# Moving large loads and the start of the score bursts into the first matmul of each group: attention and MLP on one core

## The chip, the cores and the metric

The kernel runs on one core of a Trainium2 chip. The metric is device microseconds of one execution. A run is told with a state: "fast", "slow" (over 1.5% above the fastest run of the same kernel), or "unknown" for a single look. Each experiment was timed beside the kernel before on the same chip. A ratio below is the mean time of one kernel's fast runs over the mean of the other's fast runs of the same rounds, so it is not quite the ratio of the medians that stand beside it. In the views, PE is TensorE's matmuls, PEld its weight loads, DVE is VectorE, ACT ScalarE, POOL GpSimd and SP SyncE; L340 is line 340 of that run's kernel.

## The reference

Two steps, cut to what matters. First attention for 8 batches of 8 heads, 576 positions, 64 wide, in two parts that are added: a local one (each position sees neighbours closer than 4) and one on means of 4 positions. Then an MLP on the 4,608 tokens.

```python
q_d, k_d, v_d = (t.reshape(B, H, S // 4, 4, D).mean(axis=3) for t in (q, k, v))
out_up = np.repeat(sm_attn(q_d, k_d, v_d), 4, axis=2)
mask = np.abs(pos[:, None] - pos[None, :]) < 4
out_local = softmax(where(mask, scale * q @ k.T, -1e9)) @ v
x = (out_up + out_local).transpose(0, 2, 1, 3).reshape(B * S, H * D)   # 4608 x 512
h = x @ w_in                                                            # 512 -> 2048
out = (h * sigmoid(1.702 * h)) @ w_out                                  # 2048 -> 512
```

## The kernel before

The MLP runs in nine groups of 512 tokens. A group has `mm1` (64 matmuls of 512 columns, then SiLU on ACT) and `mm2` (64 more). While group g runs, the attention of batch g+1 is put between the matmuls of `mm2`, as bursts of many small matmuls: `scores` and `scores_d` for each half of the heads (called qd 0 and 1; 104 small matmuls each), `av` (44 for each of four head pairs), `transp` (28 each). Every matmul is two TensorE instructions, a weight load and a matmul (the trace has 5,148 of each).

```python
    def mm2(g, gT, steps):
        # ... cut
        for t, ffc in order:
            for f in steps.get(n, ()):
                f()                       # a burst of attention, ahead of matmul n
            n += 1
            # ... one 512-column matmul; every 16th: copy out and store

    POS = [0, 18, 25, 32, 43, 52]         # s0, s1, av(0,1), av(2,3), tr(0,1), tr(2,3)

    for g in range(n_groups):
        b = g + 1
        # ... g == 0 cut
        elif b < B:
            if b + 1 < B:
                for qd in range(NQ):
                    load_qk(b + 1, qd)    # POOL's queue; fp32 to bf16
            prep_qk(b, 0)                 # DVE transposes
            pool_qk(b, 0)                 # POOL: sums of four
            prep_v(b, nc.gpsimd)
            if b + 1 < B:
                load_v(b + 1)             # SP's queue, 256-byte pieces
            prep_qk(b, 1)
            pool_qk(b, 1)
            prep_v4(b, nc.gpsimd)
            if b + 1 < B:
                load_v4(b + 1)            # SP's queue, 1,024-byte pieces
        gT = mm1(g)
        # ... steps from POS, cut
        mm2(g, gT, steps)
```

Note where POOL meets `load_qk(b + 1)`: in program order at the start of a group, but POOL has by then done the `prep_v4` of the group before, so it issues these loads as soon as that is finished, in the middle of the group before (in the group from 164.12 us, from 180.78 us on).

The softmax here doesn't subtract the row's maximum and nothing guards it: scores larger than these inputs give would overflow.

## Time and profile before

| | before |
|---|---|
| median of fast runs (first three / beside the changed kernel) | 368.75 / 367.67 us |
| span of the profiled run | 367.2 us |
| PE busy | 86% |
| four groups with a long gap | 40.8, 39.4, 38.8, 38.3 us |
| the group with attention and no gap, from 241.16 us | 33.6 us |

The page in 40 slices: busy tenths of PE, and the clock that TensorE was granted.

```profile
PE   0224899959978999699969997999999999999996
...
PEclk9998699977998999699989999899999999999999
```

PE has dents at slices 11, 16, 20 and 24 (counted from 0), and the clock drops at or beside some of them. The table of PE's waits (what waited, for whom: us in total, times, longest) names them:

```profile
PE sl_194 L273 <- DVE vf L517: 11.6, 1, 11.6
PE av L340 <- issue: 9.3, 4, 3.3
...
PE av L326 <- issue: 6.0, 2, 3.2
PE xt L379 <- issue: 3.3, 2, 2.4
```

"issue" means that nothing the profile shows was waited for. The chain of waits around one gap (start us, us, what; L326 and L340 are the two halves of `av`):

```profile
184.48 1.62 PE ops L492 x7
186.09 0.28 PE av L326 x20
186.38 0.19 PE av L340 x24
...
186.94 3.32 issue
190.27 0.26 PE av L340 x2
```

The table by stretches (window, length; busy us and instructions of PE, weight loads, DVE, ACT, POOL; granted clock, DMA share, GB/s) for the time around that gap, then for three groups:

```profile
183.00:187.00 4.00, 3.94 (x199) 2.52 (x197) 1.27 (x4) 3.36 (x5) 0.00 (x0) 1.00 1.14 199
187.00:190.00 3.00, 0.00 (x0) 0.00 (x0) 1.01 (x1) 0.39 (x1) 0.00 (x0) 1.00 1.09 245
190.00:194.00 4.00, 3.73 (x57) 1.46 (x61) 1.34 (x2) 0.28 (x1) 0.00 (x0) 0.57 0.64 122
```

```profile
124.75:164.12 39.37, 36.25 (x625) 17.96 (x624) 15.14 (x25) 20.90 (x32) 17.34 (x19) 0.91 0.58 122
...
202.89:241.16 38.27, 35.50 (x625) 17.51 (x624) 15.04 (x25) 20.90 (x32) 17.33 (x19) 0.96 0.64 126
241.16:274.73 33.57, 33.57 (x625) 16.96 (x624) 14.94 (x25) 20.90 (x32) 15.23 (x15) 1.00 0.47 108
```

PE did nothing for 3 us while the DMA engines were full, and then ran at 0.57 of its clock for the next 4 us. The same work takes 33.57 us where there is no gap. The queues in 183 to 191 us (packets, MB, share of the time of 16 engines) show who filled the engines: q/k on the software queue, v4 on the hardware queue, and a single packet of the queue called "instruction":

```profile
q0 software_dynamic: 446, 0.93, 62.2%
q1 hardware_dynamic: 731, 0.81, 49.7%
q8 instruction: 1, 0.02, 0.7%
```

The prologue, in the chain: v is issued at 11.61 us and lands at 24.2; the MLP starts in earnest at 40.65.

```profile
10.48 1.08 DVE qT_146 L200
...
11.61 0.72 SPq L153
...
18.41 5.81 DMA vf<-in_v_dram
...
40.65 0.58 PE hps L465
```

### The profile page before, as it was taken

The numbers are of one execution on the slowest core, as the hardware profiler recorded it, in microseconds if no ns is written. First come the engines' busy times: TensorE is split into PE (matmuls) and PEld (weight loads), VectorE is DVE, ScalarE is ACT, GpSimd is POOL, SyncE is SP. The second block draws the span as 40 slices with busy tenths as digits, with TensorE's granted clock in tenths as the row PEclk, the third lists the DMA queues.
The fourth block names the chain that finished last, engine by engine and source line by source line (L and its number), as shares of the span: only waits on it lengthen the run. The fifth ranks groups of instructions, "written<-read, shape, count | busy, mean of one in ns | idle before, by whom it ended". The sixth has DMA issues, their size and how long they took to land.

```text
span 367.2 us, 11384 instructions
## 1 busy us (share of the span) xinstructions
PE 315.8 (86%) x5148; PEld 157.5 (43%) x5148; DVE 130.3 (35%) x219; ACT 180.8 (49%) x278; POOL 134.1 (37%) x157
## 2 busy tenths in 40 slices
PE   0224899959978999699969997999999999999996
PEld 0313344533444445344535454445544454444442
DVE  4727540276034802463136513460473163000000
ACT  1322373734760668146733675267636746623621
POOL 5871077007920396009900791069009700000000
PEclk9998699977998999699989999899999999999999
DMA  7499975998894149712991099317710011002002
GB/s 126 103 183 208 210 152 80 225 216 158 167 196 102 60 91 188 174 42 65 190 206 60 32 180 199 90 54 153 151 61 30 2 61 59 2 29 87 2 29 86
DMA packets 63265, 41.37 MB, mean 113 GB/s; under 512 B 44016, under 2 KB 54000, under 8 KB 63216
## 3 DMA queue, kind: packets, MB, share of 16 engines
q1 hardware_dynamic: 54912, 27.01, 32.6%
q0 software_dynamic: 8304, 13.63, 21.0%
q8 instruction: 40, 0.66, 0.8%
q14 instruction: 9, 0.07, 0.1%
HBM read 44.83 MB, written 9.44 MB: 148 GB/s over the span
## 4 chain that ended last, share of the span: by engine, by line
PE 82%; issue 6%; DVE 5%; ACT 2%; SPq 2%; DMA 2%; POOL 1%; DVEq 0%; POOLq 0%; ACTq 0%
PE ops L492 36%; PE hps L465 34%; PE av L340 2%; PE av L326 2%; DVE y L354 2%; SPq L153 2%; PE xt L368 2%; PE sd L289 2%; DMA vf<-in_v_dram 2%; PE xt L379 1%; PE vdp L246 0%; DVE xT_84 L406 0%; DVE vb_86 L224 0%; ACT osb L500 0%; DVE xT_85 L406 0%
## 5 line engine op out<-in xcount | busy, mean ns | idle before, releaser
L492 PE MATMUL ops<-w_out_bf,gT 128*128 128x512 bf16 x576 | 137.7, 393 | 0.0
L471 ACT ACTIVATE gT<-hps 128x512 bf16<-128x512 f32 x144 | 86.0, 597 | 44.7 <-PE hps L465 44.7
L465 PEld LDWEIGHTS <-w_in_bf 128*128 128x128 bf16 x576 | 57.0, 99 | 73.4 <-issue 8.5
L492 PEld LDWEIGHTS <-gT 128*128 128x128 bf16 x576 | 54.6, 100 | 65.4 <-issue 7.0
L465 PE MATMUL hps<-xT_84,w_in_bf 128*128 128x512 bf16 x144 | 55.7, 387 | 0.9 <-DVE xT_84 L412 0.9
L465 PE MATMUL hps<-xT_85,w_in_bf 128*128 128x512 bf16 x144 | 55.7, 387 | 0.5 <-DVE xT_85 L412 0.5
L465 PE MATMUL hps<-xT_82,w_in_bf 128*128 128x512 bf16 x144 | 56.1, 390 | 0.0
L465 PE MATMUL hps<-xT_83,w_in_bf 128*128 128x512 bf16 x144 | 56.0, 389 | 0.0
L500 ACT ACTIVATE osb<-ops 128x512 f32<-128x512 f32 x36 | 21.4, 597 | 67.6 <-PE ops L492 50.2
L390 ACT COPY od<-xt 128x576 f32<-128x576 f32 x32 | 19.1, 641 | 42.8 <-PE xt L379 42.8
L314 DVE TENSOR_TENSOR es_90<-es_90,mask 128x600 bf16<-128x600 bf16 x8 | 4.3, 536 | 89.8 <-ACT es_90 L300 89.8
L354 DVE TENSOR_TENSOR y<-av,rc 128x896 bf16<-128x896 f32 x32 | 34.9, 1092 | 1.1
L352 DVE RECIPROCAL rc<-av 128x14 f32<-128x14 f32 x32 | 7.7, 240 | 29.6 <-PE av L340 29.6
L368 PE MATMUL xt<-ident,y 60*64 60x57 bf16 (+1 forms) x640 | 10.5, 201 | 3.4 <-DVE y L354 3.2
L314 DVE TENSOR_TENSOR es_92<-es_92,mask 128x600 bf16<-128x600 bf16 x8 | 4.2, 531 | 25.1 <-ACT es_92 L300 25.1
L368 PEld LDWEIGHTS <-y 60*64 60x64 bf16 x640 | 8.2, 115 | 9.0 <-DVE y L354 5.3
L379 PE MATMUL xt<-ident,y 36*64 36x36 bf16 x256 | 8.1, 188 | 3.3 <-issue 3.3
L273 PE MATMUL sl_194<-qT_146,kT_144 32*64 32x60 bf16 x40 | 0.9, 242 | 11.6 <-DVE vf L517 11.6
L224 POOL CAST vb_87<-vf 128x2560 bf16<-128x2560 f32 x4 | 9.3, 2318 | 4.1 <-DMA vf<-in_v_dram 4.1
L424 ACT ACT_TABLE_LOAD x8 | 10.3, 1283 | 0.9 <-PEq L586 0.7
L436 ACT ACT_TABLE_LOAD x8 | 10.3, 1283 | 0.1
L406 DVE TENSOR_TENSOR xT_82<-xt,od 128x570 bf16<-128x570 f32 x8 | 6.0, 752 | 9.8 <-ACT od L390 9.8
(319 smaller groups left out, 361.1 us busy)
## 6 DMA issues: line engine op xcount, KB each, us to landing
vf<-in_v_dram SPq DMA_DIRECT2D x80, 128.0 KB, 3.7
out_dram<-osb SPq DMA_DIRECT2D x36, 256.0 KB, 2.1
v_96<-in_v_dram SPq DMA_DIRECT2D x36, 192.0 KB, 6.4
w_out_bf<-in_moe_w_out_dram POOLq DMA_DIRECT2D x4, 512.0 KB, 17.8
w_in_bf<-in_moe_w_in_dram POOLq DMA_DIRECT2D x2, 512.0 KB, 7.5
w_in_bf<-in_moe_w_in_dram POOLq DMA_DIRECT2D x1, 1024.0 KB, 13.2
kb_100<-in_k_dram POOLq DMA_DIRECT2D x1, 288.0 KB, 4.6
qb_102<-in_q_dram POOLq DMA_DIRECT2D x1, 288.0 KB, 5.3
```

What stands on the lines that cost most here:

```text
L224: eng.tensor_copy(out=vbs[b % 2][:, :, :, 0:D], in_=vf[b])
L314: nc.vector.tensor_tensor(out=ev, in0=ev, in1=mask, op=ALU.mult)
L354: nc.vector.tensor_tensor(out=y, in0=ov[:, :, :, 0:D], in1=rc.to_broadcast([128, 2, 7, D]), op=ALU.mult,)
L368: nc.tensor.matmul(x[64 * j : 64 * j + 64, par, 57 * i + c0 : 57 * i + c1], lhsT=y[64 * pos : 64 * pos + 60, par, i, :], rhs=ident[64 * po ...
L379: nc.tensor.matmul(x[64 * j : 64 * j + 64, xx, 288 + 36 * c2 : 324 + 36 * c2], lhsT=y[64 * pos : 64 * pos + 36, j, 5 + c2, :], rhs=ident[6 ...
L390: nc.scalar.copy(out=od.rearrange("p (x t f) -> p x t f", x=2, f=4), in_=x[:, :, 288:360, None].to_broadcast([128, 2, 72, 4]),)
L424: nc.scalar.preload_act_table_set("exp_and_others")
L436: nc.scalar.preload_act_table_set("silu_and_others")
L465: nc.tensor.matmul(hps, lhsT=w_in_bf[:, dmc, ffc * 128 : (ffc + 1) * 128], rhs=xT[dmc][:, tok0 : tok0 + TG], start=(dmc == 0), stop=(dmc = ...
L471: nc.scalar.activation(out=gT[:, ffc, :], in_=hps, func=AF.Silu, scale=GELU_SCALE)
L492: nc.tensor.matmul(ops[t], lhsT=gT[:, ffc, t * 128 : (t + 1) * 128], rhs=w_out_bf[:, ffc, :], start=(ffc == 0), stop=(ffc == n_ffc - 1),)
L500: nc.scalar.activation(out=osb, in_=ops[t], func=AF.Copy, scale=1.0 / GELU_SCALE)
```

## The change

The intent: the queue called "instruction" moved 40 packets of 16,384 B in the kernel before, which I read as TensorE's own instruction fetches. So let the bursts, which use up instructions fast (199 matmuls in 183 to 187 us, where large ones alone are some 18 in 4 us), run when few long transfers are in flight. Three things are done. The q/k loads of the next batch go behind `pool_qk(b, 0)`, and v4 is loaded at the start of its own group. The first score burst starts in `mm1` (slot 13 of 16), and the later positions move. In the prologue and group 0, constants that are needed late are made late, and the first v load no longer waits for the q transpose.

```diff
-        F = {}
+        # iotas reordered: those of the mask first (cut)
+        return dp, dr, di
+
+    def late_constants(dp, dr, di):
         nc.vector.tensor_single_scalar(out=ident, in_=di, scalar=0.0, op=ALU.is_equal)
         # ... rv, psel (cut)
@@ attention @@
-        return [s0, s1, avn(0, 1), avn(2, 3), tr(0, 1), tr(2, 3)]
+        return [lambda: s_pe(0), lambda: s_act(0), s1, avn(0, 1), avn(2, 3), tr(0, 1), tr(2, 3)]
-    def mm1(g):
+    def mm1(g, steps):
         for ffc in range(n_ffc):
+            for f in steps.get(ffc, ()):
+                f()
-    POS = [0, 18, 25, 32, 43, 52]
+    POS = [13, 16, 35, 40, 47, 54, 62]    # 16 is the first matmul of mm2
@@ prologue @@
-    constants()
-    prep_qk(0, 0)
+    late = constants()
+    prep_1("k", 0, 0)
+    load_v(0, gate=lambda t: nc.vector.memset(t, 0.0))
+    prep_1("q", 0, 0)
     pool_qk(0, 0)
-    load_v(0, gate=lambda t: nc.vector.memset(t, 0.0))
@@ groups @@
         elif b < B:
-            if b + 1 < B:
-                for qd in range(NQ):
-                    load_qk(b + 1, qd)
+            load_v4(b)
             prep_qk(b, 0)
             pool_qk(b, 0)
+            if b + 1 < B:
+                for qd in range(NQ):
+                    load_qk(b + 1, qd)
             prep_v(b, nc.gpsimd)
             # ... load_v, prep_qk(b, 1), pool_qk(b, 1) as before (cut)
             prep_v4(b, nc.gpsimd)
-            if b + 1 < B:
-                load_v4(b + 1)
```

More of the change, by code (lines that the diff above doesn't have):

```diff
@@ L79, in constants @@
         it = dict(allow_small_or_imprecise_dtypes=True)
+        halves = [slice(0, 64), slice(64, 128)]
         for par in range(2):
-            sl = slice(64 * par, 64 * par + 64)
-            nc.gpsimd.iota(dm[sl], pattern=[[-1, 60]], base=-4 * par,
+            nc.gpsimd.iota(dm[halves[par]], pattern=[[-1, 60]], base=-4 * par,
                            channel_multiplier=1, **it)
-            nc.gpsimd.iota(dp[sl], pattern=[[114, 5], [-192, 3], [-4, 64]],
+        for par in range(2):
+            nc.gpsimd.iota(dp[halves[par]], pattern=[[114, 5], [-192, 3], [-4, 64]],
                            base=KSTART[par], channel_multiplier=1, **it)
-            nc.gpsimd.iota(di[sl], pattern=[[-1, 64]], base=0,
+        nc.gpsimd.iota(dr, pattern=[[0, 1]], base=0, channel_multiplier=1, **it)
+        for par in range(2):
+            nc.gpsimd.iota(di[halves[par]], pattern=[[-1, 64]], base=0,
                            channel_multiplier=1, **it)
-        nc.gpsimd.iota(dr, pattern=[[0, 1]], base=0, channel_multiplier=1, **it)
         for t in kdT:
@@ L194, with prep_1 @@
     qT, kT, qdT = {}, {}, {}
-    def prep_qk(b, qd):
-        for name, store, dst in (("k", kf, kT), ("q", qf, qT)):
-            tt = work.tile([128, S, 2], BF16, name=f"{name}T{qd}", tag=f"{name}T{qd}", bufs=1)
-            t32 = tt.rearrange("p t a -> p (t a)").bitcast(FP32)
-            nc.vector.transpose(
-                out=t32.rearrange("p (i c) -> p c i", c=18),
-                in_=store[b, qd].bitcast(FP32).rearrange("p (c d) -> p c d", c=18),
-            )
-            dst[b, qd] = tt
+    def prep_1(name, b, qd):
+        store, dst = {"k": (kf, kT), "q": (qf, qT)}[name]
+        tt = work.tile([128, S, 2], BF16, name=f"{name}T{qd}", tag=f"{name}T{qd}", bufs=1)
+        t32 = tt.rearrange("p t a -> p (t a)").bitcast(FP32)
+        nc.vector.transpose(
+            out=t32.rearrange("p (i c) -> p c i", c=18),
+            in_=store[b, qd].bitcast(FP32).rearrange("p (c d) -> p c d", c=18),
+        )
+        dst[b, qd] = tt
+    def prep_qk(b, qd):
+        prep_1("k", b, qd)
+        prep_1("q", b, qd)
     def pool_qk(b, qd):
@@ L421, in attention, with s_pe, s_act @@
         st = {}
-        def s0():
-            nc.scalar.preload_act_table_set("exp_and_others")
-            st["s", 0] = scores(b, 0)
-            st["d", 0] = scores_d(b, 0)
-            exp_local(0, st["s", 0])
-            exp_down(0, st["d", 0])
-            mask_local(0)
-        def s1():
-            st["s", 1] = scores(b, 1)
-            st["d", 1] = scores_d(b, 1)
-            exp_local(1, st["s", 1])
-            exp_down(1, st["d", 1])
-            nc.scalar.preload_act_table_set("silu_and_others")
-            mask_local(1)
+        def s_pe(qd):
+            st["s", qd] = scores(b, qd)
+            st["d", qd] = scores_d(b, qd)
+        def s_act(qd):
+            if qd == 0:
+                nc.scalar.preload_act_table_set("exp_and_others")
+            exp_local(qd, st["s", qd])
+            exp_down(qd, st["d", qd])
+            if qd == 1:
+                nc.scalar.preload_act_table_set("silu_and_others")
+            mask_local(qd)
+        def s1():
+            s_pe(1)
+            s_act(1)
         def avn(*hps):
@@ L506, in mm2 @@
             f()
-    POS = [0, 18, 25, 32, 43, 52]
-    POS0 = [36, 52, 64, 64, 64, 64]
+    POS = [13, 16, 35, 40, 47, 54, 62]
+    POS0 = [52, 52, 68, 80, 80, 80, 80]
     for qd in range(NQ):
         load_qk(0, qd)
-    constants()
-    prep_qk(0, 0)
+    late = constants()
+    prep_1("k", 0, 0)
+    load_v(0, gate=lambda t: nc.vector.memset(t, 0.0))
+    prep_1("q", 0, 0)
     pool_qk(0, 0)
-    load_v(0, gate=lambda t: nc.vector.memset(t, 0.0))
     prep_qk(0, 1)
@@ L527 @@
     steps = attention(0)
-    steps[0]()
-    steps[1]()
+    for f in steps[:3]:
+        f()
+    late_constants(*late)
     prep_v(0, nc.vector)
     prep_vd_pe(0)
-    for f in steps[2:]:
+    for f in steps[3:]:
         f()
@@ L538 @@
         if g == 0:
-            prep_qk(1, 0)
+            prep_1("k", 1, 0)
             load_v(1, gate=lambda t: nc.vector.memset(t, 0.0))
+            prep_1("q", 1, 0)
             pool_qk(1, 0)
@@ L544 @@
             prep_v(1, nc.gpsimd)
-            for qd in range(NQ):
-                load_qk(2, qd)
         elif b < B:
+            load_v4(b)
+            prep_qk(b, 0)
+            pool_qk(b, 0)
             if b + 1 < B:
@@ L550 @@
                     load_qk(b + 1, qd)
-            prep_qk(b, 0)
-            pool_qk(b, 0)
             prep_v(b, nc.gpsimd)
@@ L558 @@
             prep_v4(b, nc.gpsimd)
-            if b + 1 < B:
-                load_v4(b + 1)
-        gT = mm1(g)
         steps = {}
@@ L566 @@
             if g == 0:
-                steps[64].insert(0, lambda: prep_vd_pe(1))
-        mm2(g, gT, steps)
+                steps[80].insert(0, lambda: prep_vd_pe(1))
+        gT = mm1(g, steps)
+        mm2(g, gT, {n - 16: f for n, f in steps.items() if n >= 16})
         if g == 0:
+            for qd in range(NQ):
+                load_qk(2, qd)
             load_v(2)
-            load_v4(2)
 _INS = ['q', 'k', 'v', 'moe_w_in', 'moe_w_out']
```

## The prediction

> **What bounds it now.** TensorE. Chain of waits: 82% PE, 6% "issue". The 1,152 512-column matmuls step every 0.216 us, so 64 take 13.8 us. By the chain, the group from 241.16 us, with attention and no stall, takes 33.57 us. The four groups starting at 83.96, 124.75, 164.12 and 202.89 us take 40.79, 39.37, 38.77 and 38.27: together 22.9 us over 33.57.
>
> **Where that goes.** The table of PE's waits gives "issue" 19.3 us: single gaps of 3.24, 3.12, 3.32 and 2.77 us at 108.8, 147.3, 187.0 and 227.5 us, in av bursts; then the granted clock falls (0.57 in 190-192) for some 3.4 us, about 1.7 us more each. I read the gaps as instruction fetch. The DMA queue "instruction" moved 40 packets, 16 KB each; the four gaps fall at PE instruction counts exactly 1,280 = 5x256 apart. [...] By packet records, a fetch starts about 1.0 us after PE crosses a block with DMA idle, 2.0-3.3 with v loads in flight, 4.0-5.2 where the v4 and q/k loads overlap; it takes 0.9 and PE resumes 1.3 later. So 3.3 us idle, about 7 loaded, against 2.9-4.7 us between crossings in the bursts. The unstalled group has no q/k load in its bursts.
>
> **What the change does.** In steady groups (T = start of mm1): Pool now issues q/k(b+1) after pooling its first half (about T+5, before T+16.7 to T+20); v4 is issued at T+1, before T+14; v follows at about T+9. At 180-200 GB/s (windows), 3.54 MB end near T+18, before the second score burst. Arithmetic is unchanged; q/k, v and v4 still arrive in time (POOL ends about T+19 as before; first av at T+21).
> - Four long gaps and their cold clock go. But s1 to av is now 5 slots, not 7: in three groups the two crossings stand about 2.5 us apart, less than the idle 3.3, so I expect gaps of 0.5-1.2 us there[...]; about none in the group whose crossings are 4 us apart. The first of the four keeps its slow-clock start (1.4 us). Estimates: -4.6, -4.9, -4.4, -4.5 = -18.4 us, on the chain.
> - Prologue: 2.5 us of DVE constants leave the path before the first transpose, iotas for the mask come first, and v's gate no longer waits for the q transpose. v issue 11.6 to about 7.5 us, its landing 24.2 to about 20.5 (it now shares with q/k). First full mm1: 40.65 to about 37: -3.8. The two fetch gaps there (1.72, 2.39), beside the weights' loads, stay.
> - Group 0 keeps its serial tail (73 to 84); its q/k(3) load leaves it: 0 to -1.
>
> **Prediction.** 368.75 - 22.4 = 346.3 us; 8 in 10 within 340 to 354. Faster 0.96, same 0.03, slower 0.01.
>
> **What would show it.** PE "issue" from 19 to 6-9 us, no gap over 2 us after group 0; four groups at 33.6-36.5 us; no clock below 0.9 there; DMA idle or only output between T+19 and T+27; v's first issue near 7.5 us.
>
> **What would make it wrong.** The q/k and v loads together delay the fetch of the block crossed at about T+12 past T+19.5; v4 lands late, so POOL and av slip; loads in mm1 last longer than 18 us; or queue order holds v4 back. If no fetch gap goes, the cause was not DMA traffic.

-18.4 for groups 1 to 4, -3.8 for the prologue and the rest for group 0 are the -22.4. That a block is 256 instructions fits the trace before: besides the gaps that are 5 x 256 apart, PE ran 10,311 instructions (5,148 weight loads, 5,148 matmuls, 15 semaphore instructions) while the instruction queue moved 40 packets, which is one for every 258.

## The result, and the profile after

| | before | after |
|---|---|---|
| median of fast runs, same rounds | 367.67 us | 348.01 us |
| ratio, 95% interval | | 0.9471, 0.9391 to 0.955 |
| first SiLU of the MLP | 41.27 us | 36.30 us |
| group 0 (first SiLU to first SiLU) | 43.31 | 42.88 |
| groups 1 to 4 | 41.06, 39.37, 38.77, 38.27 | 36.24, 34.89, 35.31, 34.60 |
| group 5 | 33.58 | 34.47 |
| PE gaps over 0.4 us in groups 1 to 5 | 0.74, 3.24, 3.12, 3.32, 2.77 | 1.46, 0.52, 1.12, 1.54, 0.66, 0.54 |

The rows close: -4.97 (prologue) -0.43 (group 0) -16.43 (groups 1 to 4) +0.89 (group 5) is -20.94 us, and the profiled spans are 367.2 and 346.3 us.

The same slices of the page after:

```profile
PE   0444999859979998999889998999899999999995
...
PEclk9999999978999999999999999999999999999999
```

PE's waits after. (The 31 short "issue" waits of ops in this profile, 5.3 us in all, are matmuls whose records are missing: it shows 542 of the 576.)

```profile
PE sl_183 L281 <- DVE qT_148 L204: 8.8, 1, 8.8
PE ops L503 <- issue: 5.3, 31, 0.5
PE av L348 <- issue: 4.6, 3, 1.9
...
PE av L334 <- issue: 1.5, 1, 1.5
```

The chain at the longest gap that is left, and the groups by stretches:

```profile
171.07 0.28 PE av L334 x20
171.71 0.20 PE av L348 x19
171.91 1.54 issue
173.45 0.22 PE av L348 x3
```

```profile
114.52:149.41 34.89, 32.87 (x619) 17.06 (x624) 15.06 (x25) 20.69 (x32) 17.39 (x20) 1.00 0.68 138
149.41:184.72 35.31, 32.88 (x618) 17.05 (x624) 15.06 (x25) 20.70 (x32) 17.41 (x20) 1.00 0.68 136
184.72:219.32 34.60, 33.03 (x618) 17.14 (x624) 14.95 (x25) 20.79 (x32) 17.42 (x20) 1.00 0.66 139
```

The gap stands in the same code, half as long, and the clock of these groups is 1.00. The prologue after: v is issued 3.94 us earlier, and the MLP starts 4.96 us earlier.

```profile
7.67 0.72 SPq L157
...
15.14 3.50 DMA vf<-in_v_dram
...
35.69 1.44 PE hps L476 x3
```

One thing is not as planned. In the group from 149.41 us, v was in flight until 171.0 by the packet records, so the second score burst (168.7 to 169.9 us) still met full DMA engines. The queues in 166 to 169 us:

```profile
q1 hardware_dynamic: 2199, 0.55, 126.5%
```

### The profile page after: what moved, and what is told of

Same layout as the page of the kernel before. It is cut to its first block, busy times and chain, and to the rows that moved or that the text cites. A ratio compares the mean times of both kernels' runs of the same rounds, so it can differ in the third digit from the quotient of the medians.

```text
span 346.3 us, 11340 instructions
## 1 busy us (share of the span) xinstructions
PE 302.3 (87%) x5096; PEld 156.1 (45%) x5148; DVE 132.1 (38%) x219; ACT 179.9 (52%) x278; POOL 135.5 (39%) x157
## 3 DMA queue, kind: packets, MB, share of 16 engines
q0 software_dynamic: 8304, 13.63, 22.6%
## 4 chain that ended last, share of the span: by engine, by line
PE 83%; issue 5%; DVE 5%; SPq 2%; ACT 2%; DMA 1%; POOL 1%; POOLq 0%; ACTq 0%; DVEq 0%
PE hps L476 36%; PE ops L503 35%; PE av L348 2%; SPq L157 2%; DVE y L362 2%; PE av L334 2%; PE xt L376 2%; PE sd L297 2%; DMA vf<-in_v_dram 1%; PE xt L387 1%; PE vdp L254 0%; DVE xT_84 L414 0%; DVE vb_86 L232 0%; ACT osb L511 0%; DVE xT_85 L414 0%
## 5 line engine op out<-in xcount | busy, mean ns | idle before, releaser
L503 PE MATMUL ops<-w_out_bf,gT 128*128 128x512 bf16 x542 | 124.2, 379 | 5.4 <-issue 5.3
L503 PEld LDWEIGHTS <-gT 128*128 128x128 bf16 x576 | 53.8, 98 | 62.5 <-issue 0.5
L476 PE MATMUL hps<-xT_84,w_in_bf 128*128 128x512 bf16 x142 | 55.0, 387 | 1.3 <-DVE xT_84 L420 0.6
L476 PE MATMUL hps<-xT_85,w_in_bf 128*128 128x512 bf16 x143 | 55.2, 386 | 0.7 <-DVE xT_85 L420 0.6
L476 PE MATMUL hps<-xT_82,w_in_bf 128*128 128x512 bf16 x142 | 54.6, 385 | 0.1
L511 ACT ACTIVATE osb<-ops 128x512 f32<-128x512 f32 x36 | 21.6, 604 | 60.1 <-PE ops L503 43.4
L476 PE MATMUL hps<-xT_83,w_in_bf 128*128 128x512 bf16 x131 | 50.9, 389 | 0.7 <-issue 0.3
L376 PEld LDWEIGHTS <-y 60*64 60x64 bf16 x640 | 8.5, 117 | 10.3 <-DVE y L362 4.1
L437 ACT ACT_TABLE_LOAD x8 | 10.3, 1283 | 0.9 <-PEq L598 0.7
L441 ACT ACT_TABLE_LOAD x8 | 10.3, 1283 | 0.1
L218 POOL TENSOR_TENSOR pq<-kT_1572 128x576 f32<-128x576 bf16 x1 | 1.1, 1140 | 21.9 <-DVE kT_1572 L204 21.9
```

The lines of the kernel that those rows point to most:

```text
L376: nc.tensor.matmul(x[64 * j : 64 * j + 64, par, 57 * i + c0 : 57 * i + c1], lhsT=y[64 * pos : 64 * pos + 60, par, i, :], rhs=ident[64 * po ...
L437: nc.scalar.preload_act_table_set("exp_and_others")
L441: nc.scalar.preload_act_table_set("silu_and_others")
L476: nc.tensor.matmul(hps, lhsT=w_in_bf[:, dmc, ffc * 128 : (ffc + 1) * 128], rhs=xT[dmc][:, tok0 : tok0 + TG], start=(dmc == 0), stop=(dmc = ...
L503: nc.tensor.matmul(ops[t], lhsT=gT[:, ffc, t * 128 : (t + 1) * 128], rhs=w_out_bf[:, ffc, :], start=(ffc == 0), stop=(ffc == n_ffc - 1),)
L511: nc.scalar.activation(out=osb, in_=ops[t], func=AF.Copy, scale=1.0 / GELU_SCALE)
```

## The experiments

**Theory (fetch).** PE runs on from one block of 256 instructions to the next (the four long gaps before are 1,280 = 5 x 256 instructions apart). At each crossing a block is fetched by DMA (40 packets of 16,384 B before), and PE needs it at the crossing after that (the fetch from 148.11 to 149.07 us follows the crossing at 144.1, and PE waits at the next one, from 147.32 to 150.44). The gap is what the fetch takes longer than PE takes for its block. Moving the loads makes the fetch shorter.
**Rival 1 (position).** The gaps are a wait of one step, and beginning the scores earlier removes it.
**Rival 2 (one load).** Only one of the two loads does the harm.
**Rival 3 (bytes).** Any DMA traffic does it, whatever its shape.

For each run I worked out the *fetch delay*: the time from PE's first instruction past a crossing to the first record on the instruction queue. The table has the crossing in the second score burst of groups 1 to 4. It is the fetch that the gap in `av` ends on: before, the four fetches ended at 110.59, 149.07, 188.97 and 228.74 us, and PE went on at 112.00, 150.44, 190.27 and 230.23, 1.3 to 1.5 us later each time. (The delay is used for crossings in bursts only: among the large matmuls a fetch can begin before PE's own crossing, as at 57.6 us before a crossing at 61.9 in the kernel before.)

| run | in flight in the bursts | fetch delay, us | gaps in av, us | ratio to before (95%) |
|---|---|---|---|---|
| before | q/k and v4 | 4.1, 4.0, 4.3, 5.1 | 3.2, 3.1, 3.3, 2.8 | 1 |
| after | stores, end of v | 1.8, 1.3, 2.1, 1.9 | 1.5, 1.1, 1.5, none | 0.9471 (0.939 to 0.955) |
| e4 position alone | q/k and v4 | 3.7, 3.7, 4.0, 3.9 | 3.5, 3.4, 3.5, 1.6 | 0.9958 (0.990 to 1.002) |
| e5 prologue alone | q/k and v4 | 4.5, 4.1, 4.1, 4.3 | 3.8, 3.5, 3.6, 1.7 | 0.9830 (0.975 to 0.991) |
| e1 q/k moved | v4 | profile in the slow state | | 0.9896 (0.981 to 0.998) |
| e2 v4 moved | q/k | 3.5, 4.0, 4.3, 4.1 | 2.7, 3.2, 3.5, 1.6 | 0.9909 (0.983 to 0.998) |
| e3 both moved | stores, end of v | 1.5, 2.6, 1.8, 1.6 | 0.8, 1.5, 1.1, none | 0.9528 (0.948 to 0.958) |
| e8 after, q/k put back | q/k | 3.4, 3.6, 3.8, 3.7 | 3.0, 3.1, 3.2, 1.6 | 0.9821 (0.977 to 0.987) |
| e11 as e8, 256-byte pieces | q/k | 2.7, 2.9, 2.5, 3.7 | 2.9, 2.3, 2.0, 1.6 | 0.9768 (0.970 to 0.983) |

### Parts of the change alone: e1, e2, e4, e5

e1, from the kernel before:

```diff
-            if b + 1 < B:
-                for qd in range(NQ):
-                    load_qk(b + 1, qd)
             prep_qk(b, 0)
             pool_qk(b, 0)
+            if b + 1 < B:
+                for qd in range(NQ):
+                    load_qk(b + 1, qd)
```

> The kernel before with one edit: the q/k loads of the next batch are issued after the pooling of the first half instead of after the v4 pooling. Fetch theory: q/k leave the bursts, v4 (1,024-byte elements) stays in them, so a fetch starts 2.0-2.6 us after a block crossing instead of 4.0-5.2; the four long PE gaps shrink from 2.8-3.3 to 1.5-2.2 us[...]; about 353 us (-15). Rival, score position: the loads do not matter, gaps and time as before (within 3 us).

Measured: the three fast runs took 363.21, 367.45 and 363.69 us, against a median of 367.94; the profiled run was a slow one (369.82), so I read no gap from it. The gain is about 4 us where I expected 15. The packets of that profile still show that v4 now fills more of the second score burst: between the block crossing there and the end of its fetch, 663 to 1,059 packets of 1,024 B moved, against 199 to 448 in the kernel before. So e1 does not show what v4 does in the smaller share that it had before.

e2, from the kernel before:

```diff
         elif b < B:
+            load_v4(b)
@@
             prep_v4(b, nc.gpsimd)
-            if b + 1 < B:
-                load_v4(b + 1)
@@ after group 0 @@
             load_v(2)
-            load_v4(2)
```

> The kernel before with v4 loaded at the start of its own group instead of in the bursts of the group before. Fetch theory: q/k alone remain in the bursts, fetch starts 2.5-3.5 us after the crossing, gaps 2.0-3.0 us; about 360 us (-8). Rival, score position: as before. Rival, only q/k count: as before too; then the first run should take all of the gain.

Measured: 364.75 us; gaps 2.65, 3.19, 3.51 and 1.55. The gain of 3.4 us (0.9%) is less than half of the 8 that I expected, since the fetch delays (3.5 to 4.3 us) were nearly those of both loads together. So v4 beside q/k adds little.

e4, from the kernel before: only `mm1(g, steps)`, the split of the first score step and the new `POS` and `POS0`.

> The kernel before with the scores begun in the first matmul and the new step positions, all loads as before. Fetch theory: the loads still lie in the bursts, and two crossings now stand 2.5 us apart instead of 2.9, so the four gaps stay at 2.8-4 us; 366 to 372 us, no gain. Rival, score position: 16 us of gain without any load moved (about 352).

Measured: 367.32 us, no gain that is clear of noise, with three gaps of 3.4 to 3.5 us. Rival 1 falls: with the loads where they were, the new positions remove no long gap.

e5: the changed prologue and group 0 gate with the old steady groups.

> The kernel before with the constants and the v gate of the changed prologue alone. Both theories: first full mm1 at about 36 instead of 40.65 us, steady groups as before with their four long gaps; about 363 us (-5).

Measured: 363.49 us, ratio 0.983, and the first SiLU at 36.37 us as in the changed kernel (36.30). The steady groups kept their gaps. The prologue is a separate gain of 5 to 6 us, made before the first of these gaps.

### Both loads, and one put back: e3, e8

e3 is e1 and e2 together, with the old positions and the old prologue.

> The kernel before with both load moves and nothing else: old step positions, old prologue. Fetch theory: only output stores meet the bursts, gaps at most 1.2 us in three groups (crossings 2.9 us apart against an unloaded fetch of 3.3-4.0), none long, no clock drop; about 350 us, 1 to 3 us better in the steady groups than the change itself. Rival, score position needed as well: clearly above 356.

Measured: 352.45 us against 369.83, ratio 0.9528. The line of PE's waits for `av`, which was 9.3 us with a longest of 3.3 before:

```profile
PE av L340 <- issue: 4.1, 3, 1.5
```

So the two load moves alone give 4.7%, without the positions. One alone gives 1.0% (e1) and the other 0.9% (e2): the sum is far less than what both give. Rival 2 falls as well. Either load in the bursts keeps most of the time lost (for q/k the delays of e2 show it, for v4 only the time of e1 does); only when both are gone does the fetch become fast (1.5 to 2.6 us in e3, against 3.5 to 4.3 in e2). I had expected delays that add up, one part for each load, and that model fell here. I had also expected e3's steady groups to be 1 to 3 us shorter than those of the change, and they are not: groups 1 to 5 take 176.38 us in its profile and 175.51 in that of the changed kernel. So the new positions neither gave nor cost much beside the loads.

e8 is the changed kernel with one load put back:

```diff
             pool_qk(b, 0)
-            if b + 1 < B:
-                for qd in range(NQ):
-                    load_qk(b + 1, qd)
             prep_v(b, nc.gpsimd)
@@
             prep_v4(b, nc.gpsimd)
+            if b + 1 < B:
+                for qd in range(NQ):
+                    load_qk(b + 1, qd)
```

> The changed kernel with the q/k loads alone put back behind the v4 pooling, into the bursts. Fetch theory: q/k alone in the bursts with crossings 2.5 us apart: gaps back to 2.3-3.3 us in three groups, 1-2 in the others; about 357 us (+9 on the change). Rival, score position: stays at 348.

Measured: 363.83 us. PE's waits show the long gaps again:

```profile
PE av L348 <- issue: 8.7, 3, 3.2
PE av L334 <- issue: 6.3, 3, 3.0
```

The loss was larger than expected (ratio 0.9821 against the change's 0.9471: 3.5 points of some 368 us are about 13 us, where I expected 9). Three groups took 39.24, 39.55 and 38.77 us, about as long as before: in this profile each of the three gaps was followed by 3.4 or 6.8 us at half clock.

### Is it the block? e10

e10 adds 64 small matmuls, 128 PE instructions, to the kernel before, in the prologue where PE waits for v anyway. Nothing else moves.

```diff
     prep_v(0, nc.vector)
+    pad = ps_tile("pad")
+    for i in range(64):
+        nc.tensor.matmul(
+            pad[0:64, 0, 0:64], lhsT=psel[:, 0, 0, :], rhs=psel[:, 0, 0, :],
+            start=True, stop=True,
+        )
     prep_vd_pe(0)
```

> The kernel before with 64 small matmuls (128 PE instructions) added where PE waits for v in the prologue; nothing else. Fetch theory: the gaps stay at the same PE instruction counts (192 past a multiple of 256), so they move to other code: in the group from about 84 us into the third or fourth av instead of the second, next group the third av, next two the first av. Rival (a wait tied to one step, such as the second av): gaps stay in the second av of three groups and the third of the fourth. Time within 3 us of before in both.

Measured: 366.63 us (one look). I counted the weight loads ahead of each gap and doubled them, because a few matmul records were missing here and no weight load was. (PE also runs two semaphore instructions in each group, which this count leaves out: with them the 1,278 between the long gaps of the kernel before are the 1,280 of the prediction.)

| | gaps over 0.45 us in groups 1 to 4, at instruction count |
|---|---|
| before | 2748, 3002, 4280, 5558, 6836 |
| e10 | 3002, 3258, 4536, 5814, 6836, 7092 |

Each of e10's gaps is at a count of the kernel before or exactly 256 past one, although the program there had moved by 128 instructions. So the gaps moved to other code. The chain of e10 in the third of these groups has its gap inside the fourth `av`, not the second:

```profile
181.24 0.28 PE av L326 x20
181.52 0.19 PE av L340 x24
181.71 0.09 PE av L326 x11
181.80 3.11 issue
184.91 0.28 PE av L326 x9
```

A wait that belongs to a step cannot do that. Of the places that I had named, the first two and the fourth came true (the fourth group had a second gap too); in the third group both the first and the fourth `av` hold a crossing, and it was the fourth that stalled. A block of 256 instructions fits the packets too: the instruction queue moved 40 packets of 16,384 B in the kernel before and 41 in e10, which is 128 instructions longer. With crossings every 256 instructions through the gaps, the 10,311 instructions of the kernel before have 40 crossings, and 128 more make it 41.

### What in the traffic slows the fetch? e6, e7, e11

How a DMA engine chooses between its queues is not shown by any run here. To see whether the length of the pieces counts, I tried three shapes of the same q/k bytes.

e6 writes each load as four runs of 288 elements in one DMA:

```diff
-                    ap=[[1152, 128], [1, 1152]],
+                    ap=[[1152, 128], [x, 1152 // x], [1, x]],     # x = 288
```

> The kernel before; each q/k load of batches 2 and up is one DMA as before but in four runs of 288 elements per partition (packets of 576 B in the trace instead of 2,304 B). If the fetch waits for a single long element, the four gaps shrink to the 1.5-2 us of v4 alone. If it waits for a DMA's whole share of an engine, or for bytes in flight, gaps stay at 2.8-3.3 us.

This tested nothing: the packets in the trace still had 2,304 B, as many as in the kernel before (8,304 on the software queue in both), so the four runs went as one. (The 1.5-2 us "of v4 alone" was my estimate; no run shows it.) As a repeat of the kernel before it is of use: 367.25 us, gaps 3.24, 3.95, 3.32, 1.85. The fourth gap varies from run to run (2.77 and 1.85 us for the same traffic).

e7 makes four DMAs of each load, and the packets did become 576 B (18,672 on the software queue):

> The kernel before; each q/k load of batches 2 and up is four DMAs of 288 elements per partition. If the fetch waits behind one DMA's whole share of an engine, that share is now a quarter: gaps shrink to 1.5-2.2 us. If only the bytes in flight count, gaps stay at 2.8-3.3 us.

Measured (one look): 366.69 us, fetch delays 2.9, 4.4, 4.3, 3.4, gaps 1.92, 3.48, 3.63, 1.00. Two of four were untouched. As v4 was in flight too, this does not decide.

e11 is e8 (q/k alone in the bursts) with 256-byte pieces, even ones in one DMA and odd ones in another, so that no two adjacent ones are in one DMA (33,264 packets on the software queue, so these stayed apart):

```diff
+            for o, m in ((0, 5), (128, 4)) if b > 1 else ((0, 0),):
+                # pieces = t as 9 pieces of 128; out: every second one from o // 128
+                        ap=[[1152, 128], [256, m], [1, 128]]
```

> The run with q/k put back into the bursts, but its loads of batches 2 and up move 256-byte pieces (even and odd pieces in two DMAs), the same bytes at the same place. In the runs so far a fetch beside v (256-byte pieces) started 1.3 us after its crossing with the DMA engines 100% busy, beside 2,304-byte q/k pieces 3.4-3.8 us. If the length of the pieces counts: delay 1.3-2.2 us, gaps at most 1.6 us, about 350 us. If bytes in flight or the software queue count: delay 3.4 or more, gaps 3 us, about 364 us. Between: both.

Measured: 359.64 us, delays 2.7, 2.9, 2.5, 3.7. Three of the four lie between e8 (3.4 to 3.8) and what the changed kernel has beside v (1.3 to 2.1); the fourth is that of e8. The intervals of the ratios of e8 and e11 overlap, so in time the difference is not clear; in three delays of the one profile it is. Rival 3 in its plain form falls. After the change, in the group from 114.52 us, 256-byte v pieces filled the engines while the fetch was due (134 to 135.5 us, 221 GB/s) and it started after 1.3 us, with v in flight for 0.8 us more. In e8, 186 GB/s in a window as full (138.6 to 142.2 us), nearly all q/k pieces of 2,304 bytes, held it for 3.6. First the changed kernel, then e8:

```profile
q1 hardware_dynamic: 1177, 0.32, 100.2%
```

```profile
q0 software_dynamic: 320, 0.65, 107.2%
```

Full engines alone do not make the fetch slow. But short pieces do not cure it on the software queue either (2.5 to 3.7 us in e11). How much is the length and how much the queue stays open. So does how much is the end of the load: in the groups from 78.56 and 149.41 us of the changed kernel the fetch started only after the last v packet (100.24 after 99.42, 171.22 after 171.05 us).

### The gaps that are left: e9, e12

In the changed kernel `av` comes five slots after the second score burst, and in three groups the two crossings stand some 2.5 us apart (estimated from the order of instructions, at 0.216 us for a large matmul and 0.0115 for a small one: in the chains, 64 large ones take 13.81 us, the 104 of a score burst 1.23, the 44 of an `av` 0.47). That is less than even a good fetch: 1.3 to 2.1 to start, 0.9 to 1.4 to move, 1.3 to 1.6 until PE goes on. e9 spreads the bursts: the second score burst one slot earlier (34), and each head pair's `av` and transpose in a slot of its own. The text on record names other positions (33, 41, ... 66); the kernel that ran had those of this diff:

```diff
-        return [..., s1, avn(0, 1), avn(2, 3), tr(0, 1), tr(2, 3)]
+        return [..., s1, avn(0), avn(1), avn(2), avn(3), tr(0), tr(1), tr(2), tr(3)]
-    POS = [13, 16, 35, 40, 47, 54, 62]
+    POS = [13, 16, 34, 40, 44, 48, 52, 56, 59, 62, 65]
     # ... POS0: four more entries of 80 (cut)
```

> The changed kernel with the bursts spread: second score burst two slots earlier (33), then each head pair's av and transpose in a slot of its own (41, 46, 50, 54, 58, 61, 64, 66), so no two block crossings stand closer than about 3.3-3.9 us. Fetch theory: the remaining gaps of the changed kernel (1.46, 0.48, 1.12, 1.54, 0.66, 0.54) fall to 0.5 or less each; 343 to 345 us, 1% better than the change. Rival (what is left is no fetch): no gain over the change within 0.3%.

> The changed kernel again, on the chip of the spread version, for comparison: 346 to 350 us, ratio to the kernel before 0.945 to 0.95.

Measured: e9 347.37 us, ratio 0.9438 (0.9388 to 0.9488); e12, the changed kernel again, 347.48 us, ratio 0.9435 (0.9389 to 0.9481), just below the 0.945 to 0.95 that I expected. The same. The crossings of the two bursts stand 3.8 to 4.9 us apart in e9's profile, and all gaps over 0.4 us are gone from its groups 1 to 6, but no time is won:

| group | 1 | 2 | 3 | 4 | 5 | 6 |
|---|---|---|---|---|---|---|
| e12, us | 35.59 | 35.19 | 35.04 | 34.89 | 34.19 | 33.57 |
| e9, us | 35.41 | 34.40 | 34.44 | 34.44 | 34.46 | 34.37 |

Group 6 shows part of why: it had no gap to lose and its clock was 1.00 in both runs, and it is 0.80 us longer. The stretches around it, first e9, then e12:

```profile
252.40:286.70 34.30, 33.35 (x617) 16.84 (x624) 13.73 (x23) 20.83 (x32) 14.87 (x15) 1.00 0.30 67
```

```profile
253.50:287.10 33.60, 32.70 (x619) 16.96 (x624) 13.27 (x23) 20.70 (x32) 14.89 (x15) 1.00 0.28 69
```

By this one group, four more bursts cost some 0.2 us each (0.80 / 4, an estimate), and part of it may be the small "issue" at the end of a burst:

```profile
208.58 0.97 PE ops L503 x4
209.55 0.28 PE av L334 x19
209.84 0.19 PE av L348 x21
210.03 0.16 issue
```

In these profiles groups 1 to 5 are together 1.75 us shorter in e9. Group 6 gives back 0.80, and a fetch gap in the prologue is 3.21 us long instead of 2.34; in other runs with the changed prologue it takes 2.35 (e11) to 3.18 (e8), so that part may be chance. The expectation for e9 was right about the gaps, though at other positions, and wrong about the time: I had not charged for the added bursts.

## Why the prediction was right or wrong

The time was right: 348.01 us, 346.3 predicted, inside the range. It is partly luck that it came so close, for errors cancelled: groups 1 to 4 gave 2.0 us less than predicted and group 5 lost 0.89, while the prologue gave 1.2 more. Point by point:

- **Gaps are instruction fetches.** Right. The counts, the ends of the fetches and e10 show it.
- **"-4.6, -4.9, -4.4, -4.5 = -18.4 us".** Measured -4.82, -4.48, -3.46, -3.67 = -16.43. The term that was mis-sized is the gap that stays: predicted 0.5 to 1.2 us in three groups and about none in the fourth, measured 1.46, 1.12, 1.54 and 0.66. I had put an idle fetch (start after 1.0 us) against crossings 2.5 us apart; with the end of v and the output stores in flight it started after 1.3 to 2.1. For the same reason group 5 got a gap of 0.54 that I had not expected, and lost 0.89 us. PE's "issue" fell from 19.3 to 10.3 us (without the waits of ops, which are mostly missing records), not to 6 to 9.
- **Clock.** Right: no gap over 2 us after group 0, and the clock of groups 2 to 4 went from 0.91 to 0.96 to 1.00. In groups 1 to 5 of the two kernels the clock fell behind the long gaps alone: before, gaps of 2.8 to 3.3 us were followed by a reduced clock (0.57 in 190 to 194 us); those of up to 1.5 us after were not (1.00 behind each). But the other runs show that the length of one gap does not decide. Over the 3.4 to 4 us behind it, the clock was 1.00 in e2 after a gap of 3.19 us and 0.58 in e11 after one of 2.01; in e10 (one look) it was 0.57 and 0.50 after gaps of 1.61 and 1.84 us. So that the gaps of the change would leave the clock alone came true, but nothing measured beforehand had shown it.
- **"3.54 MB end near T+18, before the second score burst".** Wrong. With T the start of the group, v ended at T+21.6 in the group from 149.41 us (171.0), and at T+20.8 to T+22.6 in the others. The gain held all the same: beside what was left of v, and the stores, the fetches started after 1.3 to 2.1 us. I had counted bytes and an empty engine. That it helped to have v come last, with its 256-byte pieces, is likely but not shown: no run put another load last.
- **Prologue, -3.8.** Measured -4.97 (e5 alone: -4.90 at the first SiLU). v landed at 18.6, not 20.5 us, 11.0 us after its issue where I had put 13; what made it faster is not shown.
- **Group 0, 0 to -1.** Measured -0.43.
- **Starting the scores earlier** was priced at no gain, only at closer crossings. e4 (0.9958) agrees.

The model behind the numbers was partly wrong where the prediction did not test it: I took v4 alone to be mild and the delays to add. e1, e2 and e3 show that one load is enough to keep most of the loss.

## What to carry to other kernels

If TensorE stops for 1 to 3 us with nothing to wait for, in code that runs many small matmuls, count its instructions ahead of the gaps: gaps a multiple of 256 instructions apart, each with a packet of the instruction queue that ends shortly before it does (1.3 to 1.5 us here), point to fetches. Here they were fought by clearing *both* loads with long pieces from the bursts; clearing one was not enough. Letting the load with the short pieces come last may help too, but this is not shown. A gap of 3.3 us cost about 5 here (38.77 against 33.57 us for a group) because the clock fell too (to 0.57 for the next 4 us), so make the long gaps short first; cutting the bursts into more pieces to remove the rest won nothing here. And test parts of such a change together as well as alone: here two moves gave 1% each and 4.7% together.

## What the traces show of the fetch

- In bursts of small matmuls the fetch was not hidden: gaps of 2.77 to 3.32 us before, and still 0.5 to 1.5 us after the change.
- The fetch begun at one crossing is the one that PE waits for at the next: for the crossing at 144.1 us of the kernel before it began at 148.11 and ended at 149.07, and PE, which had stopped at 147.32, went on at 150.44.
- What a fetch takes: at crossings in and just after bursts, it started 0.5 to 1.1 us after the crossing with DMA idle (four crossings of the kernels before and after and of e8), 1.3 to 2.6 beside 256-byte v pieces and stores (the changed kernel and e3), 3.4 to 5.1 beside q/k in long pieces with or without v4 (the second score bursts; at the next crossings of the kernel before, with q/k still in flight, 1.1 to 2.8); then 0.9 to 1.9 us to move 16 KiB, and 1.2 to 1.6 us until PE went on.
- 256-byte pieces on the software queue still held a fetch for 2.5 to 3.7 us (e11), and on the hardware queue for 1.3 to 2.1 (the changed kernel). Why is not shown.
- Four adjacent runs of 576 B in one DMA went as packets of 2,304 B (e6).
- Going from large matmuls into a burst of small ones and back cost some 0.2 us for each added burst, an estimate from one group of e9 (0.80 us longer with four more bursts).
